# First batch scored in two halves, an expert order by landing, and a last part stored in four pieces

## The chip, the cores and the metric

The kernel runs on one core of a Trainium2 chip. The core has TensorE (matmuls; its weight loads are listed apart as PEld), VectorE (DVE), ScalarE (ACT), GpSimd (POOL) and SyncE (SP, which here only issues transfers), and sixteen DMA engines that carry every transfer. The metric is the device time in microseconds, the median over runs.

## The reference

Two stages, all in float32. The first is an attention between 512 tokens and 32 states for 8 batches of 8 heads (head size 64), in both directions: `softmax(x state^T / 8) state` gives the tokens' read, `softmax(state x^T / 8) x` the states' read. The two are joined to 544 rows a batch, 4352 rows of 512 in all. The second stage is a soft mixture of 8 experts with 4 slots each: `logits = rows @ phi` (512 x 32); a softmax down the rows gives the slots' inputs; each expert does `max(slot @ w1, 0) @ w2` (512 to 1024 to 512) on its 4 slots; a softmax along the 32 logits mixes the slots' outputs back to every row. The weights are 33.6 MB of the input, x is 8.4 MB, and 8.9 MB are written.

## The kernel before

The program is one list of steps, `ORDER`, that is walked once; each word is a function and its arguments (`X.2.1` is `X(2, 1)`), and a `!` has its copy done by VectorE, not ScalarE. The engines' instruction queues follow this list, so it alone sets what stands ahead of what. `HOMES` names the buffer that each tile takes in turn, and with it which older reader a transfer must wait for.

Attention, for batch b. `X` (L317) turns the x of two heads on TensorE, four blocks of 128 x 128, `xe` copies them out scaled, `S` (L330) scores all heads against the states into two banks, `sp0` and `sp1`. From there two ways run side by side. `q`, `m1`, `sub`, `x1`, `l1`, `rr`, `mul`, `aT` turn the scores (VectorE), take maxima (VectorE), subtract (GpSimd), exponentiate (ScalarE), sum (VectorE), divide (GpSimd) and turn back (VectorE): the tokens' softmax. `m2`, `e2`, `E`, `ee`, `R` do the states' softmax and its product with x. `A`/`ae` turn the tokens' softmax for later, `Lx` makes its logits `lt`.

Slots' inputs, for a pair of batches k: `mx`, `mk`, `bm`, `nme` find the running maximum, `dx` exponentiates, `dT`/`dTe` turn the result, `T`, `tt`, `Px`, `Y` add the pair's share to `y`. For the states' rows `Ls`, `Lr`, `msx`, `dsx`, `Ps`, `Ys` do the same, with `V`/`Ve` and `U`/`Ue` turning what they need; `keep` and `lkp` copy logits aside. At the end `SI` turns `y` and `SIe` writes the slots' inputs to `si_m` (L723).

Experts. `W.hf.e` (L744) is expert e's first layer for one half of the 1024 columns, four matmuls, each of which stands twice in the trace; eight of them add up in one bank. `hc`, `ht`, `hr` copy, turn and sum it. `u.k.hf.e` (L804) is the second layer for output part k of 128 columns; parts 0, 1 use the first column half of w2 and parts 2, 3 the second. `c`, `s` sum a part, `o` (L836) mixes it back to rows, `oc` (L851) copies the eight banks of a part out, four by each engine, and stores each four banks as 1 MB:

```python
n = 2 if (k, q) in HALVED else 4
if j % n == n - 1:
```

Transfers. ScalarE issues one of the first three; SP issues all others in the order of the list, into one queue. Weights land in the order of `LOADS`: most of the first layer's tiles early, with those of experts 3 and 4 of the first half taken late because their buffers still hold attention data (steps `ld`), then the second layer's. The stores follow in the same queue.

Of the kernel before, what the change touches and what calls it, by code (L numbers as in the profile page):

```python
# [52 lines left out]
srTe.6 A.5.1 windows aT.6.0 mk.2 l1.7.1 A.5.0 bm.2 nme.2 ae.5.0 R.7.0 ae.5.1 Lx.6.0 rr.7 mul.7.0 aT.6.1 R.7.1 sr.7
dx.2 A.6.0 dT.2 dTe.2! srT.7 aT.7.0 A.6.1 keep.2 mul.7.1 aT.7.1 pv.3! srTe.7 Ls.1 tt.1 D.0 T.2 Lx.6.1 Lx.7.0 Lx.7.1
mx.3 mk.3! ld.4 als.0 ld.5 ae.6.0 al.2 ae.6.1 V.1 A.7.0 bm.3 nme.3 ae.7.0! A.7.1 al.1 Lse.1 Lr.1 msx.1 dx.3 dT.3
dTe.3! al.3 ae.7.1 Px.1 Lu.1 Lus.0 Lu.2 als.1 tt.2 Ps.0 Ue.1 dsx.1 T.3 Px.2 Lu.3 Lus.1 Y.1 Ys.0 ld.6 D.1 ld.7 ld.8
# [868 lines left out]
```

## Time and profile before

| | us |
|---|---|
| median of 3 runs (lowest to highest) | 131.38 (131.15 to 132.03) |
| profiled execution | 131.39 |
| its span, first to last instruction | 129.6 |
| TensorE busy | 116.3 (90%) |
| VectorE, ScalarE, GpSimd busy | 87.4, 74.2, 44.3 |
| moved by the DMA engines | 51.76 MB, mean 399 GB/s |

The span is what the profiler saw of the program, and 1.8 us of the time lie around it. A busy share is a mean over stages that have different limits, so the tables by stretch say more than this one. For a transfer two times matter: when it is issued, and when it has landed, which is what a waiting instruction sees.

### The profile page before, as it was taken

To read this page: it belongs to the slowest core of one execution; us is meant where nothing else is said; L and a number is where in the kernel's file an instruction comes from. 1 tells how busy PE (TensorE), PEld (TensorE's weight loads), DVE (VectorE), ACT (ScalarE), POOL (GpSimd) and SP (SyncE) were. 2 spreads that over 40 slices of the span, in tenths; PEclk is the share of its full clock that TensorE was granted. 3 is DMA by queue.
4 is the path that set the end of the run, shared out by engine and by line. 5 is a ranking of instruction groups with operands and counts; after the bars stand their busy time and mean duration, and the time that the engine had idled before them with its cause. 6 is when DMAs were issued, how large, how long until landed. Compare 5 with 4: busy or idle time off the path is not lost.

```text
span 129.6 us, 4822 instructions
## 1 busy us (share of the span) xinstructions
PE 116.3 (90%) x2064; PEld 81.4 (63%) x2064; DVE 87.4 (67%) x200; ACT 74.2 (57%) x180; POOL 44.3 (34%) x60
## 2 busy tenths in 40 slices
PE   6999999999996999999999987999999999998300
PEld 3655969688665869677888672334694659476000
DVE  3049999999999999999986746049083653352700
ACT  3039999999996999999938410121203571342500
POOL 2103348563669083596664115503330000000000
PEclk9999999999999999999999999999999999999985
DMA  4999999999999999999999999999999999989593
GB/s 103 365 382 465 425 405 435 440 415 448 417 410 455 420 410 445 397 425 427 450 422 420 410 410 411 425 430 430 427 430 445 382 408 412 426 362 397 217 410 164
DMA packets 7078, 51.76 MB, mean 399 GB/s; under 512 B 784, under 2 KB 912, under 8 KB 3216
## 3 DMA queue, kind: packets, MB, share of 16 engines
q1 hardware_dynamic: 6912, 50.92, 94.4%
q10 hardware_dynamic: 144, 0.52, 1.1%
q8 instruction: 16, 0.26, 0.7%
q14 instruction: 6, 0.05, 0.1%
HBM read 42.53 MB, written 8.91 MB: 397 GB/s over the span
## 4 chain that ended last, share of the span: by engine, by line
PE 77%; DMA 12%; DVE 2%; issue 2%; ACT 1%; DVEq 0%
PE xt_ps L320 12%; DMA w<-w_in 12%; PE so_ps L813 11%; PE h_ps L750 8%; PE o L842 7%; PE sr_ps L422 7%; PE eT_ps L397 7%; PE sc L334 6%; PE an_ps L397 4%; PE spin L286 3%; PE lt L452 3%; DVE out L262 1%; PE sum_ps L832 1%; PE os L864 1%; PE hT_ps L766 1%
## 5 line engine op out<-in xcount | busy, mean ns | idle before, releaser
L356 POOL TENSOR_TENSOR q<-q,m 128x512 f32<-128x512 f32 x16 | 16.7, 1049 | 23.2 <-DVE m L352 12.4
L265 ACT ACTIVATE xt<-xt_ps 128x512 f32<-128x512 f32 x30 | 17.0, 616 | 6.3 <-PE xt_ps L320 6.3
L373 POOL TENSOR_TENSOR q<-q,rr 128x512 f32<-128x512 f32 x16 | 16.6, 1049 | 4.2 <-ACT e L389 1.9
L750 PE MATMUL h_ps<-w,si_m 128*32 128x512 f32 x128 | 14.8, 594 | 1.0 <-DMA w<-w_in 0.7
L320 PE MATMUL xt_ps<-ident,x 128*128 128x128 f32 x112 | 15.6, 276 | 0.0
L813 PE MATMUL so_ps<-w,h_m 128*32 128x128 f32 x432 | 14.3, 274 | 0.0
L813 PEld LDWEIGHTS so_ps<-w,h_m 128*32 128x32 f32 x432 | 11.7, 110 | 3.7 <-issue 3.1
L320 PEld LDWEIGHTS xt_ps<-ident,x 128*128 128x128 f32 x112 | 12.5, 141 | 1.6 <-DMA x<-x_in 0.8
L262 DVE COPY out<-o 128x512 f32<-128x512 f32 x15 | 9.4, 685 | 5.4 <-PE o L842 5.4
L384 DVE TENSOR_REDUCE nm<-sc 128x1 f32<-128x512 f32 x16 | 10.6, 663 | 1.5 <-PE sc L334 1.5
L389 ACT ACTIVATE e<-sc,nm 128x512 f32<-128x512 f32 x16 | 11.4, 723 | 0.1
L842 PE MATMUL o<-lt_all,so_r 32*128 32x512 f32 x64 | 11.2, 615 | 0.0
L262 ACT COPY out<-o 128x512 f32<-128x512 f32 x17 | 8.9, 597 | 4.0 <-PE o L842 4.0
L347 DVE STREAM_TRANSPOSE q<-sc 128x512 f32<-128x512 f32 x16 | 11.0, 692 | 0.2 <-PE sc L334 0.2
L397 PE MATMUL eT_ps<-ident,e 128*128 128x128 f32 x64 | 10.2, 281 | 1.0 <-issue 0.9
L397 PEld LDWEIGHTS eT_ps<-ident,e 128*128 128x128 f32 x64 | 7.0, 140 | 6.2 <-ACT e L389 4.2
L378 DVE STREAM_TRANSPOSE aT<-q 128x512 f32<-128x512 f32 x16 | 10.7, 687 | 0.3
L750 PEld LDWEIGHTS h_ps<-w,si_m 128*32 128x32 f32 x128 | 5.7, 110 | 7.9 <-issue 5.3
L359 ACT ACTIVATE q<-q 128x512 f32<-128x512 f32 x16 | 10.6, 660 | 0.0
L352 DVE TENSOR_REDUCE m<-q 128x16 f32<-128x512 f32 x16 | 10.5, 663 | 0.0
L362 DVE TENSOR_REDUCE ls<-q 128x16 f32<-128x512 f32 x16 | 10.4, 653 | 0.0
L262 ACT COPY eT<-eT_ps 128x512 f32<-128x512 f32 x16 | 9.6, 606 | 1.3 <-PE eT_ps L397 1.2
(138 smaller groups left out, 198.0 us busy)
## 6 DMA issues: line engine op xcount, KB each, us to landing
...
w<-w_in SPq DMA_DIRECT2D x9, 1024.0 KB, 15.1
out_x<-out SPq DMA_DIRECT2D x7, 1024.0 KB, 7.0
...
x<-x_in SPq DMA_DIRECT2D x2, 1024.0 KB, 14.6
x<-x_in SPq DMA_DIRECT2D x2, 512.0 KB, 7.1
w_half<-w_in SPq DMA_DIRECT2D x4, 256.0 KB, 15.5
w_an<-w_in SPq DMA_DIRECT2D x2, 512.0 KB, 10.6
```

The lines of the kernel that those rows point to most:

```text
L262: (dve.tensor_copy if Z["dve"] else act.copy)(out, in_)
L265: (dve.tensor_scalar_mul if Z["dve"] else act.mul)(out, in_, by)
L320: pe.transpose(p[:, P * j : P * j + P], xg[b, g][:, j, :], ident)
L347: dve.transpose(r[f"q{h}"], r[f"sp{h}"])
L356: pool.tensor_tensor(v, v, R[b][f"m1{h}"].broadcast_to([P, 16, NS]), op=ALU.subtract)
L373: pool.tensor_tensor(v, v, R[b]["rr"][:, 16 * h : 16 * h + 16].broadcast_to([P, 16, NS]), op=ALU.mult)
L378: dve.transpose(r[f"aT{h}"], r[f"q{h}"])
L389: act.activation(r[f"e2{h}"], r[f"sp{h}"], AF.Exp, bias=r[f"nm2{h}"], accum_out=ls[:, b % 2, 32 + h, 0:1])
L397: pe.transpose(p[:, j, :], r[f"{src}{h}"][:, P * j : P * j + P], ident)
L750: pe.matmul(h_ps[hf][32 * kt : 32 * kt + 32, :], si_m[kt // 2][:, 256 * (kt % 2) + 32 * e : 256 * (kt % 2) + 32 * e + 32], wt[1, hf, e, kt ...
L813: pe.matmul(so[k][32 * i : 32 * i + 32, :], h_m[hf][:, 256 * i + 32 * e : 256 * i + 32 * e + 32], wt[2, c, e, 4 * hf + i][:, col : col + n ...
L842: pe.matmul(o[j], so_r[hf][rows, col : col + 128], lt_all[rows, 4 * q : 4 * q + 4, :].rearrange("p b s -> p (b s)"), start=True, stop=True,)
```

## The change

The first batch's input is laid out by halves of 256 tokens: SP loads the states' head and groups 0 and 1 of the first half, ScalarE groups 2 and 3 of it, SP the second half. New steps `Xa`, `xa`, `Sa`, `qa`, `ma`, `sa` turn, scale, score, turn, reduce and subtract a half t at a time. `w1_part` counts the experts that are left, so that they may come in any order, and experts 3 and 4 of the first half come last. The last output part is stored in four pieces of 512 KB. The three turns that kept TensorE busy ahead of `SI` (`spin.3`) stand at the end. The list of steps and the buffers' turns are new throughout.

```diff
@@ ORDER, the list of steps: its start, the first expert layer, its end
-X.0.0 xe.0.0! X.0.2 X.0.1 X.0.3 xe.0.2 xe.0.3 xe.0.1! S.0 X.1.0 xe.1.0 m2.0.0 q.0.1 q.0.0 X.1.1 xe.1.1 X.1.2 m1.0.1
+Xa.0.1 xa.0.1! Xa.0.0 xa.0.0 Xa.1.1 xa.1.1! Xa.1.0 xa.1.0 Sa.0 qa.0.0 ma.0.0 Sa.1 qa.1.0 X.1.1 xe.1.1 X.1.0 xe.1.0
...
-tt.3 Y.2 Wd We Ve.1 Ps.1 Px.3 Y.3 Ys.1 spin.3 SI SIe W.0.0 W.0.1 lkp.1 W.0.2 W.0.3 W.0.4 W.0.5 cm.2 W.0.6 W.0.7
+Ys.1 SI We SIe W.0.0 cm.0 W.0.1 W.0.2 W.0.5 ld.8 ld.9 ld.10 W.0.6 W.0.7 W.0.3 ld.11 cx.0 W.0.4 hc.0 W.1.0 lkp.1!
...
+oc.3.1.0 oc.3.1.1! oc.3.1.2 oc.3.1.3! spin.3
...
-HALVED = ((0, 0),)
+HALVED = ((0, 0), (3, 0), (3, 1))
...
-    first = 2 * NJ * D
     xs_a = big_tile("x0_a")
     xs_b = big_tile("x0_b")
-    stT_sb = xs_b[:, first : first + 8 * P].rearrange("p (q g a b n) -> p q g a b n", q=4, g=2, a=2, b=2)
+    stT_sb = xs_b[:, F:].rearrange("p (q g a b n) -> p q g a b n", q=4, g=2, a=2, b=2)
     phi_sb = cp.tile([P, 4, NS], F32, name="phi_sb")
-    head = first + 2 * P
+    quarter, head = 4 * P, 6 * P
     nc.sync.dma_start(xs_a[:, 0:head], x0[:, 0:head])
-    act.dma_start(xs_a[:, head : head + 2 * first], x0[:, head : head + 2 * first])
-    nc.sync.dma_start(xs_b[:, 0:first], x0[:, head + 2 * first :])
-    st_head = xs_a[:, first : first + 2 * P].rearrange("p (g a b n) -> p g a b n", g=2, a=2, b=2)
+    act.dma_start(xs_a[:, head : head + quarter], x0[:, head : head + quarter])
+    nc.sync.dma_start(xs_b[:, 0:F], x0[:, head + quarter :])
+    st_head = xs_a[:, quarter:head].rearrange("p (g a b n) -> p g a b n", g=2, a=2, b=2)
+    x0_half = [
+        [t.rearrange("p (g j c) -> p g j c", g=2, j=2) for t in (xs_a[:, 0:quarter], xs_a[:, head : head + quarter])],
+        [t.rearrange("p (g j c) -> p g j c", g=2, j=2) for t in (xs_b[:, 0:quarter], xs_b[:, quarter:F])],
+    ]
     xg = {}
-    for g, t in enumerate((xs_a, xs_a[:, head:], xs_a[:, head + first :], xs_b)):
-        xg[0, g] = t[:, 0:first].rearrange("p (j c) -> p j c", j=NJ)
+
+    def x_at(b, g, j):
+        return xg[b, g][:, j] if b else x0_half[j // 2][g // 2][:, g % 2, j % 2]
+
...
+        def Xa(t, p):
+            r = R[0]
+            r[f"xp{t}{p}"] = x = bank([P, S], f"xt_ps0_{t}{p}")
+            for i in range(4):
+                pe.transpose(x[:, P * i : P * i + P], x_at(0, 2 * p + i // 2, 2 * t + i % 2), ident)
+
+        def xa(t, p):
+            r = R[0]
+            r[f"xt{t}{p}"] = half(f"xt0_{t}{p}")
+            scale(r[f"xt{t}{p}"], r[f"xp{t}{p}"], 0.125)
+
+        def Sa(t):
+            r = R[0]
+            n = S // 2
+            for h in range(2):
+                if t == 0:
+                    r[f"sp{h}"] = bank([P, S], f"sc0_{h}")
+            for g in range(4):
+                for h in range(2):
+                    pe.matmul(
+                        r[f"sp{h}"][32 * g : 32 * g + 32, n * t : n * t + n],
+                        st_t(0, g)[64 * h : 64 * h + 64, :],
+                        r[f"xt{t}{g // 2}"][64 * h : 64 * h + 64, n * (g % 2) : n * (g % 2) + n],
+                        start=True,
+                        stop=True,
+                    )
+
+        def qa(t, h):
+            r = R[0]
+            if t == 0:
+                r[f"q{h}"] = half(f"q0_{h}")
+                r[f"qv{h}"] = r[f"q{h}"].rearrange("p (k n) -> p k n", n=NS)
+                r[f"m1{h}"] = sm.tile([P, 16, 1], F32, tag=f"m1{h}", name=f"m1_0_{h}")
+            c = slice(S // 2 * t, S // 2 * (t + 1))
+            dve.transpose(r[f"q{h}"][:, c], r[f"sp{h}"][:, c])
+
+        def ma(t, h):
+            r = R[0]
+            k = slice(8 * t, 8 * t + 8)
+            dve.tensor_reduce(out=r[f"m1{h}"][:, k], in_=r[f"qv{h}"][:, k], axis=AX.X, op=ALU.max)
+
+        def sa(t, h):
+            r = R[0]
+            k = slice(8 * t, 8 * t + 8)
+            v = r[f"qv{h}"][:, k]
+            pool.tensor_tensor(v, v, r[f"m1{h}"][:, k].broadcast_to([P, 8, NS]), op=ALU.subtract)
...
-            if e == 0:
+            i0 = h_ps[hf] is None
+            if i0:
                 h_ps[hf] = bank([P, 512], f"h_ps{hf}")
+            w1_left[hf] -= 1
             for kt in range(4):
                 pe.matmul(
                     h_ps[hf][32 * kt : 32 * kt + 32, :],
                     si_m[kt // 2][:, 256 * (kt % 2) + 32 * e : 256 * (kt % 2) + 32 * e + 32],
                     wt[1, hf, e, kt],
-                    start=(e == 0),
-                    stop=(e == E - 1),
+                    start=i0,
+                    stop=(w1_left[hf] == 0),
                 )
...
+    x0 = xs[0].reshape(P, 4, 2, 2 * P).transpose(0, 2, 1, 3).reshape(P, 2, F)
-        "x0_in": con(_np.concatenate([xs[0, :, 0:512], sts[:, 0:256], xs[0, :, 512:]], axis=1)),
+        "x0_in": con(_np.concatenate([x0[:, 0, 0:512], sts[:, 0:256], x0[:, 0, 512:], x0[:, 1]], axis=1)),
```

Nearly all rows of the list differ; three places are shown as they were built. On TensorE the program starts with the first batch (`xt_ps` are turns, `sc` scores; x0_a and x0_b hold its input). Before:

```order
L320 MATMUL xt_ps0_0_138<-ident_87,x0_a_66 128x128 x4
L320 MATMUL xt_ps0_2_145<-ident_87,x0_a_66 128x128 x4
L320 MATMUL xt_ps0_1_150<-ident_87,x0_a_66 128x128 x4
L320 MATMUL xt_ps0_3_155<-ident_87,x0_b_67 128x128 x4
L334 MATMUL sc0_0_166<-xt0_0_143,x0_a_66 32x512
L334 MATMUL sc0_1_167<-xt0_0_143,x0_a_66 32x512
L334 MATMUL sc0_0_166<-xt0_1_164,x0_a_66 32x512
L334 MATMUL sc0_1_167<-xt0_1_164,x0_a_66 32x512
```

Now:

```order
L391 MATMUL xt_ps0_01_138<-ident_87,x0_a_66 128x128 x4
L391 MATMUL xt_ps0_00_145<-ident_87,x0_a_66 128x128 x4
L391 MATMUL xt_ps0_11_152<-ident_87,x0_b_67 128x128 x4
L391 MATMUL xt_ps0_10_159<-ident_87,x0_b_67 128x128 x4
L406 MATMUL sc0_0_166<-xt0_00_150,x0_a_66 32x256
L406 MATMUL sc0_1_167<-xt0_00_150,x0_a_66 32x256
L406 MATMUL sc0_0_166<-xt0_00_150,x0_a_66 32x256
L406 MATMUL sc0_1_167<-xt0_00_150,x0_a_66 32x256
```

The four turns still stand ahead of the scores, and the scores now go by 256 tokens, the first half for all groups before the second.

On TensorE at the first expert layer (`w_3276800`, `w_3538944`, `w_3801088` are experts 0 to 2, `w_5111808` and `w_5373952` experts 3 and 4, `w_0` and `w_524288` experts 5 to 7), before, from expert 2 on:

```order
L750 MATMUL h_ps0_1616<-w_3801088_756,si_m0_1319 32x512 x2
L750 MATMUL h_ps0_1616<-w_3801088_756,si_m1_1321 32x512 x2
L750 MATMUL h_ps0_1616<-w_5111808_1457,si_m0_1319 32x512 x2
L750 MATMUL h_ps0_1616<-w_5111808_1457,si_m1_1321 32x512 x2
L750 MATMUL h_ps0_1616<-w_5373952_1564,si_m0_1319 32x512 x2
L750 MATMUL h_ps0_1616<-w_5373952_1564,si_m1_1321 32x512 x2
L750 MATMUL h_ps0_1616<-w_0_124,si_m0_1319 32x512 x2
L750 MATMUL h_ps0_1616<-w_0_124,si_m1_1321 32x512 x2
L750 MATMUL h_ps0_1616<-w_0_124,si_m0_1319 32x512 x2
L750 MATMUL h_ps0_1616<-w_0_124,si_m1_1321 32x512 x2
L750 MATMUL h_ps0_1616<-w_524288_126,si_m0_1319 32x512 x2
L750 MATMUL h_ps0_1616<-w_524288_126,si_m1_1321 32x512 x2
```

Now:

```order
L805 MATMUL h_ps0_1623<-w_3801088_1227,si_m0_1458 32x512 x2
L805 MATMUL h_ps0_1623<-w_3801088_1227,si_m1_1460 32x512 x2
L805 MATMUL h_ps0_1623<-w_0_124,si_m0_1458 32x512 x2
L805 MATMUL h_ps0_1623<-w_0_124,si_m1_1460 32x512 x2
L805 MATMUL h_ps0_1623<-w_0_124,si_m0_1458 32x512 x2
L805 MATMUL h_ps0_1623<-w_0_124,si_m1_1460 32x512 x2
L805 MATMUL h_ps0_1623<-w_524288_126,si_m0_1458 32x512 x2
L805 MATMUL h_ps0_1623<-w_524288_126,si_m1_1460 32x512 x2
L805 MATMUL h_ps0_1623<-w_5111808_1539,si_m0_1458 32x512 x2
L805 MATMUL h_ps0_1623<-w_5111808_1539,si_m1_1460 32x512 x2
L805 MATMUL h_ps0_1623<-w_5373952_1589,si_m0_1458 32x512 x2
L805 MATMUL h_ps0_1623<-w_5373952_1589,si_m1_1460 32x512 x2
```

Experts 3 and 4 have moved behind 5, 6 and 7.

On VectorE at the end of the attention, from the last transpose of the tokens' softmax on (`an` and `lt` are copies out of banks, `mx` the last pair's maximum), before:

```order
L378 STREAM_TRANSPOSE aT7_1_1408<-q7_1_1123 128x512
L265 TENSOR_SCALAR mk_3_1410<-nm_all_105 128x1
L580 STREAM_TRANSPOSE tt_1_1418<-t_ps1_1181 128x128
L665 STREAM_TRANSPOSE D0_1420<-ds0_1304 128x32
L468 TENSOR_REDUCE mx_3_1451<-lt_6_1355 128x1
L265 TENSOR_SCALAR mk_3_1410<-mask_97,mx_3_1451 128x4
L532 TENSOR_REDUCE nm_all_105<-bm_ps3_1473 128x1
L262 COPY an7_1476<-an_ps7_0_1468 128x16x32
L644 TENSOR_REDUCE lr1_1486<-lr1_1486 128x1
L500 TENSOR_TENSOR nm_all_105<-lr1_1486,nm_all_105 128x1
L262 COPY dT_3_1500<-dT_ps3_1497 128x256
```

Now:

```order
L384 STREAM_TRANSPOSE aT7_1_1414<-q7_1_1166 128x512
L268 COPY an6_1436<-an_ps6_0_1400 128x16x32
L268 COPY lt_all_103<-lt_6_1438 128x256
L521 TENSOR_REDUCE mx_3_1475<-lt_6_1438 128x1
L268 COPY an7_1483<-an_ps7_0_1470 128x16x32
L585 TENSOR_REDUCE nm_all_105<-bm_ps3_1485 128x1
L268 COPY an7_1483<-an_ps7_1_1478 128x16x32
L633 STREAM_TRANSPOSE tt_2_1503<-t_ps2_1417 128x128
L577 SCALAR_TENSOR_TENSOR y_85<-y_85,al_all_106,px_ps1_1494 128x128
L268 COPY srN1_1531<-v_ps1_1465 128x512
L697 TENSOR_REDUCE lr1_1533<-lr1_1533 128x1
L553 TENSOR_TENSOR nm_all_105<-lr1_1533,nm_all_105 128x1
```

Copies of an6 and lt stand between that transpose and the maximum now, two of an7 around the running maximum, and one of srN after it; two of dT are gone from this engine.

## Rows read from the trace of the kernel before

**Rows 1.** the page, part 2: DMA share in 40 slices, in tenths.

```profile
DMA  4999999999999999999999999999999999989593
```

**Rows 2.** windows: us, busy time of each engine, PEclk, DMA share, GB/s.

```profile
10.00:15.00 5.00, 5.00 (x62) 3.56 (x61) 5.00 (x11) 5.00 (x12) 2.10 (x2) 1.00 1.05 447
...
75.00:80.00 5.00, 4.07 (x33) 2.82 (x32) 3.31 (x11) 0.42 (x1) 1.26 (x3) 1.00 1.01 408
```

**Rows 3.** timeline of PE at the first expert layer: start, us, what.

```profile
75.44 3.91 PE L750 MATMUL h_ps<-w,si_m 128*32 128x512 f32 x32 [0.28 <-DVE si_m L723]
...
80.10 5.36 PE L750 MATMUL h_ps<-w,si_m 128*32 128x512 f32 x48 [0.74 <-DMA w<-w_in]
```

**Rows 4.** chain of waits, whole span: start, us, what.

```profile
64.99 15.07 DMA w<-w_in
```

**Rows 5.** timeline of the first batch's scores and their first reader.

```profile
7.52 1.81 PE L334 MATMUL sc<-xt,x_a 64*32 64x512 f32 x16
...
9.36 0.69 DVE L384 TENSOR_REDUCE nm<-sc 128x1 f32<-128x512 f32 x1 [1.47 <-PE sc L334]
```

**Rows 6.** groups by line and form: busy, mean ns, idle before.

```profile
L347 DVE STREAM_TRANSPOSE q<-sc 128x512 f32<-128x512 f32 x16 | 11.0, 692 | 0.2 <-PE sc L334 0.2
...
L304 DVE STREAM_TRANSPOSE G_sb<-g_ps 128x256 f32<-128x256 f32 x2 | 0.8, 423 | 0.0
...
L262 DVE COPY an<-an_ps 128x512 f32<-128x512 f32 x2 | 1.4, 680 | 0.0
...
L262 DVE COPY dT<-dT_ps 128x256 f32<-128x256 f32 x2 | 0.8, 419 | 0.3 <-PE dT_ps L555 0.3
```

**Rows 7.** timeline of DVE at the end of the attention.

```profile
68.25 0.42 DVE L468 TENSOR_REDUCE mx<-lt 128x1 f32<-128x256 f32 x1 [0.25 <-PE lt L452]
...
75.20 0.48 DVE L723 TENSOR_TENSOR si_m<-si_ps,rl 128x32 f32<-128x32 f32 x4 [0.48 <-PE si_ps L705]
```

**Rows 8.** the last load: issue, us to landing; then PE's column-1 run.

```profile
87.10 0.33 SPq L201 DMA_DIRECT2D w<-w_in  x1
...
w<-w_in SPq DMA_DIRECT2D x1, 512.0 KB, 18.7
...
106.94 2.83 PE L813 MATMUL so_ps<-w,h_m 128*32 128x128 f32 x96
```

**Rows 9.** chain of waits, from 117 us to the end.

```profile
117.26 0.30 DVE so_sb L262
...
118.99 1.13 PE o L842 x6
...
120.12 1.27 DVE out L262 x2
```

**Rows 10.** timeline of SP, the last stores' issues.

```profile
119.75 0.33 SPq L873 DMA_DIRECT2D out_s<-out_s  x1
...
121.84 1.15 SPq L857 DMA_DIRECT2D out_x<-out  x2
```

**Rows 11.** DMA issues from 119.75, 121.84 and 122.66: size, us to landing.

```profile
out_s<-out_s SPq DMA_DIRECT2D x1, 256.0 KB, 3.0
...
out_x<-out SPq DMA_DIRECT2D x1, 1024.0 KB, 4.4
...
out_x<-out SPq DMA_DIRECT2D x1, 1024.0 KB, 6.0
```

**Rows 12.** windows around the last stores' start, columns as before.

```profile
121.50:122.00 0.50, 0.00 (x0) 0.00 (x0) 0.50 (x2) 0.23 (x1) 0.00 (x0) 1.00 0.14 53
...
122.40:122.60 0.20, 0.00 (x0) 0.00 (x0) 0.19 (x1) 0.00 (x0) 0.00 (x0) 1.00 0.00 0
...
122.60:122.80 0.20, 0.00 (x0) 0.00 (x0) 0.00 (x0) 0.00 (x0) 0.00 (x0) 1.00 1.25 532
```

**Rows 13.** windows while 512 KB and while 1 MB stores move.

```profile
109.00:110.00 1.00, 1.00 (x44) 1.00 (x40) 0.00 (x0) 0.00 (x0) 0.00 (x0) 1.00 1.07 434
...
115.00:116.00 1.00, 1.00 (x46) 1.00 (x40) 0.05 (x1) 0.06 (x1) 0.00 (x0) 1.00 1.03 434
```

More of the change, by code (lines that the diff above doesn't have):

```diff
@@ L53 @@
[L53 to L56, printed above, removed]
-tt.3 Y.2 Wd We Ve.1 Ps.1 Px.3 Y.3 Ys.1 spin.3 SI SIe W.0.0 W.0.1 lkp.1 W.0.2 W.0.3 W.0.4 W.0.5 cm.2 W.0.6 W.0.7
@@ new lines @@
+qa.0.1 ma.1.0 sa.0.0 sa.1.0 X.1.3 xe.1.3 m2.0.1 X.1.2 qa.1.1 ma.0.1 xe.1.2 ma.1.1 m2.0.0 U.0 sa.0.1 S.1 sa.1.1
+x1.0.0 l1.0.0 m2.1.1 q.1.0 G.0 e2.0.1 E.0.1 e2.0.0 x1.0.1 m2.1.0 m1.1.0 sub.1.0 ee.0.1 X.2.0 xe.2.0 X.2.3 xe.2.3
+E.0.0 ee.0.0 l1.0.1 q.1.1 rr.0 X.2.1 mul.0.1 xe.2.1 m1.1.1 X.2.2 xe.2.2 R.0.0 e2.1.0 Ge.0 e2.1.1 Ue.0 R.0.1 sr.0 S.2
+m2.2.1 x1.1.0 aT.0.1 E.1.0 ee.1.0 e2.2.1 m2.2.0 E.1.1 X.3.1 X.3.2 xe.3.1 xe.3.2 q.2.0 X.3.3 xe.3.3 m1.2.0 sub.1.1
+E.2.1 X.3.0 mul.0.0 aT.0.0 xe.3.0 q.2.1 srT.0 l1.1.0 x1.1.1 ld.0 l1.1.1 R.1.0 m1.2.1 sub.2.0 S.3 m2.3.0 sub.2.1
@@ new lines @@
+X.4.1 rr.1 e2.2.0 E.2.0 ee.2.1 ee.1.1 ee.2.0 xe.4.1 q.3.0 m2.3.1 Lx.0.0 srTe.0 x1.2.1 R.1.1 sr.1 mul.1.0 aT.1.0
+m1.3.0 mul.1.1 aT.1.1 sub.3.0 Lx.0.1 R.2.0 x1.2.0 A.0.1 X.4.0 A.0.0 e2.3.0 e2.3.1 ae.0.0 X.4.3 xe.4.3 srT.1 srTe.1!
+q.3.1 R.2.1 Lx.1.0 Lx.1.1 ae.0.1 xe.4.0 E.3.1 mx.0 m1.3.1 l1.2.0 mk.0 X.4.2 xe.4.2 A.1.0 X.5.0 keep.0 sub.3.1 l1.2.1
+rr.2 ld.1 sr.2 bm.0 nme.0 x1.3.0 S.4 ae.1.0 x1.3.1 l1.3.0 dx.0 l1.3.1 E.3.0 mul.2.0 aT.2.0 ee.3.0 X.5.1 xe.5.1
+ee.3.1 X.5.2 xe.5.2 A.1.1 dT.0 m2.4.1 X.5.3 rr.3 srT.2 m2.4.0 q.4.1 mul.3.0 m1.4.1 R.3.0 mul.3.1 R.3.1 sub.4.1
@@ new lines @@
+xe.5.0 xe.5.3 S.5 ae.1.1 dTe.0 e2.4.0 T.0 srTe.2 A.2.0 aT.3.0 q.4.0 e2.4.1 E.4.1 x1.4.1 sr.3 srT.3 mul.2.1 srTe.3
+X.6.3 ee.4.1 X.6.1 A.3.0 ae.2.0 al.0 m1.4.0 X.6.2 E.4.0 q.5.0 xe.6.1 aT.3.1 m2.5.1 tt.0 sub.4.0 x1.4.0 A.3.1 Lx.2.0
+aT.2.1 ae.3.0 ee.4.0 Lx.2.1 R.4.0 R.4.1 m1.5.0 sub.5.0 l1.4.0 q.5.1 xe.6.3 l1.4.1 rr.4 pv.1! x1.5.0 X.6.0 m1.5.1
+Lx.3.0 xe.6.2 xe.6.0 ae.3.1 sr.4 Lx.3.1 e2.5.1 Ls.0 Lse.0 S.6 mul.4.1 Px.0 E.5.1 m2.5.0 aT.4.1 e2.5.0 mx.1 ee.5.1
+mk.1 X.7.3 Y.0 E.5.0 A.2.1 ee.5.0 q.6.0 sub.5.1 x1.5.1 m2.6.0 q.6.1 l1.5.0 xe.7.3 ae.2.1 X.7.2 l1.5.1 R.5.0 R.5.1
@@ new lines @@
+mul.4.0 aT.4.0 keep.1 xe.7.2 m2.6.1 X.7.1 xe.7.1 m1.6.1 sub.6.1 X.7.0 xe.7.0 bm.1 nme.1 dx.1 Lr.0 rr.5 msx.0 m1.6.0
+e2.6.0 mul.5.0 S.7 q.7.0 srT.4 e2.6.1 dT.1 m2.7.0 m2.7.1 E.6.0 dTe.1 E.6.1 dsx.0 q.7.1 ee.6.0 mul.5.1 aT.5.0 m1.7.1
+sr.5 V.0 ee.6.1 Ve.0 R.6.0 aT.5.1 Lx.4.0 R.6.1 x1.6.1 ld.2 sub.6.0 x1.6.0 e2.7.1 srTe.4 sub.7.1 e2.7.0 x1.7.1 T.1
+m1.7.0 ld.3 als.0 Lx.4.1 Lx.5.0 Lx.5.1 srT.5 srTe.5 E.7.0 pv.2! tt.1 E.7.1 l1.6.0 A.5.0 ee.7.0 sub.7.0 A.4.0 mx.2
+mk.2 bm.2 l1.6.1 rr.6 A.5.1 D.0 mul.6.0 Lu.0 x1.7.0 lkp.0 ae.4.0 ee.7.1 nme.2 ae.5.0 sr.6 l1.7.0 l1.7.1 rr.7 srT.6
@@ new lines @@
+aT.6.0 R.7.0 R.7.1 sr.7 keep.2 dx.2 srTe.6! mul.6.1 A.4.1 dT.2 aT.6.1 pv.3 U.1 A.6.0 srT.7 mul.7.0 ae.5.1 dTe.2
+aT.7.0 mul.7.1 aT.7.1 ae.4.1 T.2 ld.4 ae.6.0! Lx.6.0 Lx.6.1 Lx.7.0 Lx.7.1 keep.3! al.1 al.2 windows Lu.1 srTe.7 V.1
+A.7.0 mx.3 mk.3 A.7.1 ae.7.0! bm.3 nme.3 Lus.0 dx.3 ae.7.1! Px.1 tt.2 Ue.1 Ps.0 Ls.1 Lse.1 A.6.1 ae.6.1 dT.3 dTe.3
+Y.1 Ve.1! Lr.1 ld.5 Lu.2 al.3 msx.1 als.1 Px.2 Ys.0 dsx.1 D.1 T.3 Ps.1 tt.3 Lu.3 Y.2 ld.6 ld.7 Px.3 Lus.1 Wd Y.3
+Ys.1 SI We SIe W.0.0 cm.0 W.0.1 W.0.2 W.0.5 ld.8 ld.9 ld.10 W.0.6 W.0.7 W.0.3 ld.11 cx.0 W.0.4 hc.0 W.1.0 lkp.1!
@@ new lines @@
+cm.2 cd.0 ht.0 cm.1 ld.12 cx.1 cb.0 hz W.1.1 W.1.2 hr.0 u.1.0.0 u.1.0.1 u.1.0.2 W.1.3 W.1.4 W.1.5 W.1.6 W.1.7 hc.1
+u.0.0.0 u.0.0.1 u.0.0.2 cd.1 u.1.0.3 ht.1 u.1.0.4 cx.2 hr.1 u.0.0.3 u.0.0.4 u.0.0.5 ld.13 u.0.0.6 u.0.0.7 u.0.1.0
+u.0.1.1 cb.1 u.0.1.2 u.0.1.3 u.1.0.5 ld.14 u.0.1.4 u.0.1.5 u.0.1.6 u.0.1.7 u.1.0.6 u.1.0.7 c.0 s.0 u.1.1.0 o.0.0!
+u.1.1.1 ld.15 oc.0.0.0 o.0.1 cd.2 cb.2 u.1.1.2 u.1.1.3 u.1.1.4 u.1.1.5 u.1.1.6 u.1.1.7 oc.0.1.0 oc.0.1.1 oc.0.1.2
+oc.0.1.3 oc.0.0.1! c.1! u.2.0.0 u.2.0.1 oc.0.0.2 oc.0.0.3! s.1 os.0 o.1.0! u.3.0.0 oc.1.0.0 oc.1.0.1! u.2.0.2
@@ new lines @@
+u.3.0.1 u.2.0.3 oc.1.0.2 oc.1.0.3! o.1.1 oc.1.1.0! oc.1.1.1 oc.1.1.2! u.2.0.4 u.2.0.5 u.2.0.6 u.2.0.7 u.2.1.0
+oc.1.1.3 u.2.1.1 u.2.1.2 u.2.1.3 u.2.1.4 u.2.1.5 u.2.1.6 u.2.1.7 c.2 u.3.0.2 u.3.0.3 s.2! u.3.0.4 o.2.0 oc.2.0.0
+oc.2.0.1! oc.2.0.2 oc.2.0.3! u.3.0.5 o.2.1 oc.2.1.0 oc.2.1.1! u.3.0.6 u.3.0.7 u.3.1.0 oc.2.1.2! u.3.1.1 u.3.1.2
+u.3.1.3 u.3.1.4 u.3.1.5 u.3.1.6 u.3.1.7 c.3! oc.2.1.3 s.3! os.1 o.3.0! o.3.1! oc.3.0.0! oc.3.0.1 oc.3.0.2 oc.3.0.3!
+oc.3.1.0 oc.3.1.1! oc.3.1.2 oc.3.1.3! spin.3
@@ L70 @@
     big="""
-0 1 2 3 4 0 2 3 1 4 0 2 3 1 4
+0 1 2 3 4 0 2 3 4 1 0 2 3 4 1
 """,
@@ L319, in X @@
             for j in range(NJ):
-                pe.transpose(p[:, P * j : P * j + P], xg[b, g][:, j, :], ident)
+                pe.transpose(p[:, P * j : P * j + P], x_at(b, g, j), ident)
         def xe(b, g):
@@ L736, in attention_soft_moe @@
         )
-        h_ps = [None, None]
+        h_ps, w1_left = [None, None], [E, E]
         h_m, h_sb, hT = [None, None], [None, None], [None, None]
```

39 lines of the change are left out of this document (5 added, 34 removed), and 8 rows, old and new, of the table b.

## The prediction

> **What bounds the kernel now.** I read the page's DMA line first [rows 1]: from the second slice of 3.2 us on, the sixteen DMA engines are busy 9 tenths or more, and they fall off only in the last five slices. The windows say what stands beside that. In 10 to 15 us VectorE and ScalarE are full (5.00 of 5.00 us) and TensorE's clock is granted in full, 1.00, which is the level of 2.4 GHz; in 75 to 80 us VectorE, ScalarE and GpSimd are half idle and TensorE works 4.07 of 5 us, while the DMA share is still 1.01 [rows 2]. So there are two clocks in this kernel. One is the compute: attention until 75, then experts. The other is one stream of bytes, loads first and stores behind them, on engines that hardly rest between 3 and 113 us. The reader should ask of each part of the change which of the two it moves.
>
> The chain of waits at the seam is a load: issued at 64.99, landed at 80.06 [rows 4]. TensorE's timeline shows what hung on it: 32 matmuls of the first expert layer from 75.44 on, then 0.74 us of idle until that load, then 48 more without a stop [rows 3]. The last load is issued at 87.10 and lands 18.7 us later, at 105.8; TensorE reads its column half of the second layer from 106.94 on [rows 8], a slack of 1.1 us. From there the chain goes over TensorE to the last expert at 117.26, the last products from 118.99 and VectorE's last copies from 120.12 [rows 9], and to the two stores of 1 MB issued from 121.84 on [rows 10]. The second is issued 0.33 us before that row's end, at 122.66, and lands 6.0 us later, at 128.7 [rows 10, 11]. The span ends 0.9 us behind it.
>
> **The change part by part.** The sum is made against the profiled execution: span 129.6 us, 131.39 us in all, 0.01 over the median of 131.38.
>
> *First batch in halves.* The bytes are the same. TensorE must now turn both halves before it scores the first (Sa.0 stands behind Xa.1.0), so the score starts about when it did, at 7.3 to 7.5, but its first half is half of the old 1.81 us [rows 5]: VectorE can start near 8.3 instead of 9.36, by this estimate 1.1 us earlier. It then pays for four more instructions (the four that become eight): a transpose of 256 columns takes 423 ns against 692 for 512 [rows 6], so two transposes that become four cost 4 x 0.423 - 2 x 0.692 = 0.31 us, and the two maxima, taken alike, another 0.31. That leaves 0.5 us of lead on an engine that is full from there to the end of the attention. On GpSimd two subtractions become four, at an engine that is busy 2.10 of 5 us [rows 2].
>
> *New order of the attention.* Nearly every step stands elsewhere; the total per engine hardly changes. One place can be priced. Between the last attention transpose and the maximum of the last group, VectorE now has two copies that were on ScalarE or later: one of an_ps (0.68 [rows 6]) and the 256-column copy of lt (0.42). In the old order that maximum, at 68.25, followed 0.25 us of idle [rows 7], so the cover is thin and at least 0.42 lies on the path that ends with si_m at 75.20 [rows 7]. I set lead and toll against each other: between +0.5 and -1.5, taken as zero, since the start's gain is nearly the toll's size.
>
> *Late experts last.* The tiles of experts 3 and 4 land last. Before, expert 4 stood fifth and TensorE waited 0.74 us for it; now three experts that landed long ago stand between, at 5.36/6 = 0.89 us each [rows 3]. From 75.44 on, seven experts take to 81.7, and expert 4 has landed at 80.06. The stall goes: 0.74 by the row of idle, 80.10 - 75.44 - 4 x 0.89 = 1.1 by the pace of the later run. I take 0.9. What is late next is the last load: with 0.9 less, TensorE would come to the second column half at 106.0, still behind 105.8, and the tile of that last load is for expert 7, which stands after parts for seven others. So it does not wait there.
>
> *Four stores instead of two.* The first 512 KB need two copies, one on each engine, instead of four: VectorE's first ends near 120.75 [rows 9], so its store can go near 120.9 instead of 121.84, 1.0 us earlier. Each store adds an issue of 0.33 us on SP [rows 10], which has nothing else to do. Whether smaller stores move slower: while halves of 512 KB moved the DMA took 434 GB/s, and while full ones moved 434 [rows 13]. I take zero; the bounds are zero and one more issue each, 0.7. The Trainium skill (DMA: Bandwidth & Descriptors, Rules for kernel authors) asks for at least 1 MiB per DMA for full bandwidth, which speaks against this split; the equal rates here do not bear it out for 512 KB, and by it the gain below would only shrink.
>
> *The three warm-up turns* go from before the experts to the very end of PE's queue. There si_m waited for VectorE, not for them; at the end nobody waits for them.
>
> *The sum.* On the compute's clock: 0.9 + 1.0 = 1.9 us earlier first store of the last part. But the DMA engines must be free for it. The out_s store issued at 119.75, a quarter of a megabyte, needed 3.0 us and landed at 122.75; the next megabyte, issued at 121.84, landed at 126.2, 3.5 us later [rows 11], where 1 MB takes 2.4 us at 434 GB/s. So at most 1.0 to 1.1 us of the slowest engine's time can be won. The windows bound it from below: the share is 0.14 from 121.5 on, zero only in 122.4 to 122.6, and full again behind 122.6 [rows 12]. A few engines were still working off old stores until about 122.3, and for these the pause was 0.4 us. The gain is between 0.4 and 1.1; I take 0.8, nearer the landings, because a landing is what ends the run. 131.39 - 0.8 = **130.6 us**, against the median the same.
>
> The Trainium skill (Perfetto Trace Analysis, DMA Optimizations) says that splitting transfers lets the task end sooner if DMA engines are generally idle. The share near 1.0 up to 113 us and the pause of 0.4 us agree with reading it as a limit here.
>
> **The rivals.** *The compute's clock is the only one.* If the laggard engines are less behind in the new run, because stores two and three come earlier too and nothing is refilled late, all 1.9 us pass: 129.5, and 129.2 with a part of the lead. For it: in 121.5 to 122 most engines were idle (0.14). Against it: the few that were not decide a landing. It decides if out_s lands before about 121.7 instead of 122.75. Chance 0.20.
>
> *The new order makes the expert layer late.* In the last 8 us of attention VectorE now has copies of an three times (0.68 each), of lt (0.42) and of v's result (0.68), 3.1 us, where it had one of an and two of dT, 1.5 us [rows 6]. ScalarE has three copies ahead of the last dT, estimated at 0.5 each from the same rows. If all of this lies on the chain to si_m, that is 1.6 + 1.5 = 3.1 us, the first store goes at 121.84 - 1.9 + 3.1 = 123.0, and with 6.85 us from issue to the last landing, as before, the end is 1.2 later: 132.6. It costs from the point at which si_m is later than 75.2 by more than 1.9 us. For it: the old chain there had half a microsecond of idle at each link and no more. Against it: work before that point got lighter by the same copies. Chance 0.13.
>
> *Nothing is won.* The stall goes but SP's issues, smaller rows and an engine that lags as before eat it: 131.2 to 131.5. Chance 0.14. The forecast has the rest, 0.53, with its own range of 130.2 to 131.0.
>
> **How the numbers follow.** A time within 1% of 131.38 (130.07 to 132.69) can't be told from no change by these measurements. Faster by over 1%: nearly all of the first rival and a tail of the forecast, 0.18 + 0.08 = 0.26. Slower by over 1%: the larger part of the second, 0.10. The rest, 0.64, is the same. The range is 129.4 to 132.2: it leaves out the lower edge of the first rival and the upper part of the second.
>
> **What would show it.** Right: no idle of TensorE ahead of a matmul of h_ps; VectorE's first score transpose near 8; si_m within 1 us of 75.2; last loads landing at 105 to 106 as before; four stores from about 120 on, and between the landing of out_s and the last landing no pause, so that the end is 4.9 us behind out_s. The DMA share has no window at zero before the last store. Wrong: si_m later than 77; a new wait for a load in the second layer; or an out_s that lands below 122, which means that the engines' lag was not fixed and the first rival holds.

## The result and the profile after

The changed kernel took 130.12 us (median of 10 runs, 129.82 to 130.58) against 131.19 us of the kernel before, measured again beside it: a ratio of 0.9918 (95% interval 0.9895 to 0.9941), 1.07 us less. A second measurement, beside three of the kernels below, gave 0.9896 (0.9867 to 0.9926). The profiled execution that is read here is the longest of the ten: it took 130.58 us, with a span of 128.8.

The page's DMA line after, in 40 slices of 3.2 us; it answers to [rows 1]:

```profile
DMA  4999999999999999999999999999999999999991
```

The fall in the last five slices is gone: the sixteen DMA engines are busy up to the last slice. Two windows around the last stores say the same (columns as in [rows 12]):

```profile
121.50:122.00 0.50, 0.00 (x0) 0.00 (x0) 0.07 (x1) 0.00 (x0) 0.00 (x0) 1.00 1.05 426
...
122.40:122.60 0.20, 0.00 (x0) 0.00 (x0) 0.00 (x0) 0.00 (x0) 0.00 (x0) 0.50 1.20 492
```

Where the share was 0.14 and then zero, it is 1.05 and 1.20; the lowest half microsecond between 119 and 124 us has 0.61. The stores of the last part are now issued by SP (start, us, count) at

```profile
119.08 0.34 SPq L928 DMA_DIRECT2D out_s<-out_s  x1
120.04 2.77 SPq L912 DMA_DIRECT2D out_x<-out  x4
```

and the transfers issued at 119.08 and, as the last of the four, at 121.82 land after (size, us from issue to landing)

```profile
out_s<-out_s SPq DMA_DIRECT2D x1, 256.0 KB, 3.8
...
out_x<-out SPq DMA_DIRECT2D x1, 512.0 KB, 5.8
```

So the first store of the last part goes 1.8 us earlier than in [rows 10] (120.04 for 121.84), but out_s lands at 122.88, where it landed before (122.79), and the last landing is at 127.66 instead of 128.67: 1.0 us. TensorE and VectorE at the two places that the prediction named, start and length first:

```profile
8.98 0.67 PE L406 MATMUL sc<-xt,x_a 64*32 64x256 f32 x16 [0.69 <-DVE q L421]
...
76.29 8.21 PE L805 MATMUL h_ps<-w,si_m 128*32 128x512 f32 x72 [0.42 <-DVE si_m L776]
```

```profile
8.38 0.45 DVE L421 STREAM_TRANSPOSE q<-sc 128x256 f32<-128x256 f32 x1 [0.39 <-PE sc L406]
...
76.04 0.49 DVE L776 TENSOR_TENSOR si_m<-si_ps,rl 128x32 f32<-128x32 f32 x4
```

The idle for a load in the expert layer [rows 3] is gone: 72 matmul records in one piece (each product stands twice in the trace). VectorE turns the first scores at 8.38 (its first reading of them was at 9.36, [rows 5]). And `si_m` is 0.84 us later than in [rows 7].

### The profile page after: what moved, and what is told of

Same layout as the page of the kernel before. It is cut to its first block, busy times and chain, and to the rows that moved or that the text cites. A ratio compares the mean times of both kernels' runs of the same rounds, so it can differ in the third digit from the quotient of the medians.

```text
span 128.8 us, 4863 instructions
## 1 busy us (share of the span) xinstructions
PE 115.7 (90%) x2080; PEld 83.6 (65%) x2080; DVE 88.6 (69%) x206; ACT 74.1 (58%) x178; POOL 44.7 (35%) x62
## 4 chain that ended last, share of the span: by engine, by line
PE 54%; DVE 17%; ACT 16%; issue 5%; POOL 2%; DVEq 1%; POOLq 0%
PE so_ps L868 12%; PE h_ps L805 11%; PE o L897 7%; ACT xt L271 4%; PE spin L292 3%; ACT q L365 3%; DVE nm L437 3%; PE sc L340 3%; DVE q L353 3%; ACT e L442 2%; DVE m L358 2%; ACT eT L268 2%; DVE aT L384 2%; PE an_ps L450 2%; ACT an L268 2%
## 5 line engine op out<-in xcount | busy, mean ns | idle before, releaser
L362 POOL TENSOR_TENSOR q<-q,m 128x512 f32<-128x512 f32 x14 | 14.7, 1049 | 15.7 <-DVE m L358 9.2
L868 PE MATMUL so_ps<-w,h_m 128*32 128x128 f32 x432 | 15.1, 275 | 0.0
L268 ACT COPY out<-o 128x512 f32<-128x512 f32 x18 | 9.5, 596 | 7.4 <-PE o L897 7.4
L805 PEld LDWEIGHTS h_ps<-w,si_m 128*32 128x32 f32 x128 | 8.6, 110 | 4.1 <-issue 3.2
L897 PE MATMUL o<-lt_all,so_r 32*128 32x512 f32 x64 | 10.3, 629 | 0.0
L353 DVE STREAM_TRANSPOSE q<-sc 128x512 f32<-128x512 f32 x14 | 9.8, 697 | 0.1
L450 PE MATMUL eT_ps<-ident,e 128*128 128x128 f32 x64 | 9.7, 280 | 0.0
L450 PE MATMUL an_ps<-ident,aT 128*128 128x128 f32 x64 | 9.5, 277 | 0.0
L358 DVE TENSOR_REDUCE m<-q 128x16 f32<-128x512 f32 x14 | 9.2, 661 | 0.1
```

The costliest lines, as they stand in the source:

```text
L268: (dve.tensor_copy if Z["dve"] else act.copy)(out, in_)
L362: pool.tensor_tensor(v, v, R[b][f"m1{h}"].broadcast_to([P, 16, NS]), op=ALU.subtract)
L450: pe.transpose(p[:, j, :], r[f"{src}{h}"][:, P * j : P * j + P], ident)
L805: pe.matmul(h_ps[hf][32 * kt : 32 * kt + 32, :], si_m[kt // 2][:, 256 * (kt % 2) + 32 * e : 256 * (kt % 2) + 32 * e + 32], wt[1, hf, e, kt ...
L868: pe.matmul(so[k][32 * i : 32 * i + 32, :], h_m[hf][:, 256 * i + 32 * e : 256 * i + 32 * e + 32], wt[2, c, e, 4 * hf + i][:, col : col + n ...
L897: pe.matmul(o[j], so_r[hf][rows, col : col + 128], lt_all[rows, 4 * q : 4 * q + 4, :].rearrange("p b s -> p (b s)"), start=True, stop=True,)
```

## Experiments

Two theories stood against each other. In the forecast, called the stream theory below, the DMA engines' stream sets the end (by the slowest of the sixteen engines), and time won by the products counts only while that stream has a pause. In its rival, the compute theory, every part's gain reaches the end and the parts add.

**The parts, one by one.** Four kernels took the change apart.

```diff
# a1: before
-HALVED = ((0, 0),)
+HALVED = ((0, 0), (3, 0), (3, 1))
# a2: before, with w1_part as in the change
-W.0.0 W.0.1 lkp.1 W.0.2 W.0.3 W.0.4 W.0.5 cm.2 W.0.6 W.0.7
+W.0.0 W.0.1 lkp.1 W.0.2 W.0.5 W.0.6 W.0.7 cm.2 W.0.3 W.0.4
# a3: before, with both
# a4: the change, without both
-HALVED = ((0, 0), (3, 0), (3, 1))
+HALVED = ((0, 0),)
-W.0.2 W.0.5 ld.8 ld.9 ld.10 W.0.6 W.0.7 W.0.3 ld.11 cx.0 W.0.4
+W.0.2 W.0.3 ld.8 ld.9 ld.10 W.0.4 W.0.5 W.0.6 ld.11 cx.0 W.0.7
```

a1, stores alone. 

> The kernel before with the last part in four stores of 512 KB and nothing else. Stream theory (the forecast: the slowest DMA engine sets the end, and what a part wins counts only until that engine has no pause left): the first store of the last part goes near 120.9 instead of 121.84, the pause behind out_s (1.0 us on the slowest engine) closes, and the end is 0.8 to 1.0 us earlier: nearly the whole gain of the change by itself, ratio 0.992 to 0.994. Compute theory (the parts add, each by the time it takes from the products' clock): half of the measured 1.1, ratio 0.995 to 0.997. Small rows are slow: no gain, 0.999 to 1.003.

a2, late experts alone. 

> The kernel before with experts 3 and 4 taken last in the first half of the first layer and nothing else. The wait of 0.74 us for expert 4 goes, all later products come 0.7 to 0.9 earlier. Stream theory: the stores of 1 MB go at 121.0 and 121.8 instead of 121.84 and 122.66, out_s lands near 122.7 as before, and the end is 0.7 to 0.9 earlier, ratio 0.993 to 0.995. Compute theory: 0.4 to 0.5 of the measured 1.1, ratio 0.996 to 0.997. A third: the wait only moves to another load, ratio 0.999 to 1.001, and the trace shows an idle of TensorE ahead of a later product.

a3, both. 

> The kernel before with both the four stores and experts 3 and 4 last, in the old order of the attention and the old loads at the start. Stream theory: no more than either alone, since the slowest engine's pause is only 1.0 us: ratio 0.991 to 0.993, the time of the change itself, although the first store goes near 120.0. Compute theory: 1.7 us earlier, ratio 0.986 to 0.988. If the new attention order costs something in the change, this kernel is faster than the change by that.

a4, neither. 

> The changed kernel with both undone: stores of 1 MB and experts in order; what is left is the first batch in halves and the new order of attention and products. In the change the first products of the expert layer came 0.85 us later than before (76.29 for 75.44), but the products of the output came apart in pairs and made that good (last products at 118.31 for 118.99 with the stall gone). Stream theory: TensorE waits 0.3 us for expert 4, last products near 118.6, first store near 121.5: some 0.3 to 0.8 earlier, ratio 0.994 to 0.998. The attention order as a loss: 0.85 later, ratio 1.003 to 1.007. Compute theory: 0.3 to 0.4, ratio 0.997.

Measured, as ratios to before: a1 0.9967 (0.9951 to 0.9982), a2 0.9938 (0.9908 to 0.9969), a3 0.9945 (0.9919 to 0.9971), a4 0.9938 (0.9918 to 0.9959). The stores alone won less than the stream theory gave them and fell where the compute theory had them. a2's ratio is one that the stream theory gave, but its interval reaches both. a3 and a4 speak against the compute theory, whose ratios lie outside their intervals, though a3 won a little less than the stream theory had and a4 a little more: both edits together won no more than the late experts alone, and the new order without either won as much. The three single gains sum to 1.6% (0.33, 0.62, 0.62), and the whole change won 0.8 to 1.0%. The intervals are 0.3 to 0.6% wide, so the sum speaks for parts that don't add, without proving it; the runs below are sharper.

TensorE's timeline at the expert layer shows the late-expert edit apart from the rest. First a2, then a4:

```profile
75.65 7.91 PE L752 MATMUL h_ps<-w,si_m 128*32 128x512 f32 x69 [0.28 <-DVE si_m L723]
```

```profile
75.36 3.91 PE L805 MATMUL h_ps<-w,si_m 128*32 128x512 f32 x32 [0.42 <-DVE si_m L776]
80.29 3.21 PE L805 MATMUL h_ps<-w,si_m 128*32 128x512 f32 x28 [1.01 <-DMA w<-w_in]
```

In a2 no idle is left; in a4 the wait for expert 4 is back, with 1.01 us. It is the longer the earlier `si_m` is, because the load lands when it lands: 0.74 us in before, 0.97 in b4 and 1.25 in a1, where the first product goes at 75.44, 75.38 and 74.82 and the load has landed near 80 in all of them.

**Fewer bytes.**

```diff
# b1 in the change, b4 in before
+if (k, q) != (1, 1):
     nc.sync.dma_start(out_x[k, q][:, part], ...)
```

b1, the change. 

> The changed kernel without the store of 1 MB of part (1, 1), which is never written; nothing else differs, and no engine waits for that store. Stream theory: the slowest engine reaches out_s 2.4 us earlier, so the last four stores move as soon as they are issued: from 120.04 with 1.2 us until the first byte and 4 x 1.24 us, an end near 126.3 instead of 127.7, 1.3 us below the change, ratio to before 0.981 to 0.984. Compute theory: the end hangs on the last copies, which do not move: ratio 0.990 to 0.993, as the change.

b4, before. 

> The kernel before without the store of 1 MB of part (1, 1). Stream theory: in before the slowest engine already paused ahead of the last two stores, so 2.4 us less of stream bring only what lag that engine still had at the end: 0.72 us between the first and the last of its sixteen landings, ratio 0.994 to 0.997. If the bytes alone set the time: 2.4 us, ratio 0.982. If the products alone: 1.000.

b1: 0.990 (0.988 to 0.9919). b4: 0.9997 (0.9982 to 1.0012). Both went against the stream theory as I had put it, and both fell where the compute theory had them (0.990 to 0.993 and 1.000): a megabyte less, 2.4 us of stream, bought the change some 0.2 us and before nothing. For b4 that means that before did not end by its stream at all. b1 has out_s issued at 118.46, and it landed after

```profile
out_s<-out_s SPq DMA_DIRECT2D x1, 256.0 KB, 3.6
```

that is at 122.09, only 0.8 us before the change's. A transfer's landing stands in the trace as sixteen shares, which I take to be one of each engine. Fifteen of them were there at 120.51 (in the change at 122.03); the last one came 1.58 us later. So the missing megabyte freed fifteen engines and not the slowest. The end, 126.99, is 4.90 us behind that landing, as the forecast had it. What else stood at nearly the same place, the next runs say.

**A later last part.** These kernels make products of the last part more than once, between out_s and the first store.

```diff
# b2 (DELAY 4) and b3 (DELAY 12), in the change
-for j in range(NJ):
+for j in [0] * (DELAY if (k, q) == (3, 0) else 0) + list(range(NJ)):
# c2, in the change
-for j in range(NJ):
+for j in list(range(NJ)) * (2 if (k, q) == (3, 0) else 1):
```

b2. 

> The changed kernel with the first product of the last part (3, 0) made five times instead of once, ahead of that part's other products and behind those of out_s: four repeats, about 1.1 us on TensorE by 1.14 us for a group of four. Stream theory: the last part's first store goes at 121.1 instead of 120.0, its first byte could move at 122.3, and the slowest engine is busy until 122.9: no loss or nearly none, ratio to before 0.991 to 0.995. Compute theory: 1.1 us later than the change, ratio 0.999 to 1.002.

b3. 

> As the run with four repeats, but twelve of them: about 3.4 us. Stream theory: the first store goes at 123.4, its first byte at 124.6, 1.8 us behind the point at which the slowest engine is free; the end is 1.5 to 1.9 later than the change, ratio to before 1.003 to 1.007. Compute theory: 3.4 later, ratio 1.016 to 1.019.

b2 took 1.0117 (1.0092 to 1.0142) and b3 1.1176 (1.1141 to 1.1210). The delays were mis-sized, so these two decide nothing between the theories: b2's first store went at 124.17, about 3.2 us late by its out_s (issued at 120.04, where the change has 0.96 us between the two), and b3's at 137.50. (b2's profiled execution took 134.18 us where four others took 132.35 to 132.81; its expert layer began late, at 77.25.) Repeats of one product are dear, which the last section tells. They gave a number all the same. With the DMA engines idle by then, the last landing came 7.02 us behind the first store in both (131.19 - 124.17, 144.52 - 137.50). That is what four stores of 512 KB need when nothing is ahead of them; I call it the drain. (The expectations of b1 to b3 count 1.2 us from an issue to its first byte, which no run shows: in b3, with the engines idle, the DMA share is zero up to 138.3 and 1.03 in the next 0.2 us, 0.8 us behind the issue.)

From this, after those runs, came the drain theory: **the end is the later of two times**, the first store plus the drain, and the stream's own end. c2 repeats the delay with four products on four different groups of rows. It was run with c1 (the change, with `HALVED` back to `((0, 0),)`), c3 (all halves in stores of 512 KB, `HALVED = tuple((k, q) for k in range(4) for q in range(2))`) and c4, the change as it is.

c1. 

> The changed kernel with the last part in two stores of 1 MB again; start, attention and experts stay as changed. Drain theory (formed after the last runs: the end is the later of two times, the first store of the last part plus 6.8 to 7.0 us, and the slowest DMA engine, which in the change is 0.6 us behind that): the first store goes at 120.9 instead of 120.04, which with 6.85 gives 127.75 for 127.66, 0.1 later; ratio to before 0.991 to 0.994. Compute theory: 0.85 later, ratio 0.998. Stream theory: as the change, 0.992.

c2. 

> The changed kernel with the four products of the last part's first half made twice in their own order, so that they overlap as they do once: 1.14 us on TensorE ahead of the last part, out_s untouched. Drain theory: 0.6 of it is slack, so 0.5 later than the change, ratio to before 0.994 to 0.998. Compute theory: 1.1 later, ratio 1.000. Stream theory: not later, 0.992. If the repeats cost more than 1.14 (as the repeats of one product did), the issue of the first store says how much.

c3. 

> The changed kernel with every half of every part in stores of 512 KB: five stores of 1 MB become ten. By 1.22 to 1.24 us for 512 KB and 2.44 for 1 MB in the change's landings the rows cost nothing or 0.04 per MB, 0.2 us in all, on an engine with 0.6 us over the drain: ratio 0.991 to 0.995. Should halves be clearly slower than 1 MB (a tenth less, as a rule of at least 1 MB per transfer would suggest), 5 MB lose 1.2 us: ratio 1.001.

c4. 

> The changed kernel as it is, for a time on the same chip as the three beside it and a second profile. Ratio 0.989 to 0.995. If the 0.85 us by which its expert layer began later than before was a loss of the new attention order, the first product of the expert layer stands near 76.3 again; if it was chance of one execution, it stands between 74.8 and 76.3 as in the others.

c1 0.9934 (0.9897 to 0.9971), c2 0.9916 (0.9885 to 0.9947), c3 0.9889 (0.9858 to 0.9920), c4 0.9896 (0.9867 to 0.9926), all on one chip. c1 and c4 are where the drain theory had them, and c3 is just below its range. c2 missed its range (0.994 to 0.998) and came out as the stream theory had it; but that range was made for a delay of 1.14 us with 0.6 of it free, and the delay was smaller. The compute theory's ratios for c1 and c2 lie outside the intervals, c1's narrowly. c2 beside c4 is the sharpest pair. SP's rows of c4, and the transfer of its last store, issued at 120.81:

```profile
118.08 0.34 SPq L928 DMA_DIRECT2D out_s<-out_s  x1
119.03 2.77 SPq L912 DMA_DIRECT2D out_x<-out  x4
```

```profile
out_x<-out SPq DMA_DIRECT2D x1, 512.0 KB, 6.5
```

The same of c2, whose last store is issued at 122.49:

```profile
118.89 0.34 SPq L928 DMA_DIRECT2D out_s<-out_s  x1
120.70 2.77 SPq L912 DMA_DIRECT2D out_x<-out  x4
```

```profile
out_x<-out SPq DMA_DIRECT2D x1, 512.0 KB, 5.2
```

c2 issues 1.81 us behind its out_s instead of 0.95, so the delay is 0.86 us. By the compute theory that is 0.66%, a ratio of 0.996, outside c2's interval, or 130.89 us, above all six of c2's times (129.93 to 130.86); it cost 0.15 us in the medians (130.18 for 130.03), which can't be told from nothing, nor from the 0.26 that the drain theory leaves of 0.86. Between these two executions the first store moved by 1.67 us and the last landing by 0.43 (127.29 to 127.72): the transfer waits out the difference in the queue, 6.5 us instead of 5.2. In c4 the stream runs on while nothing is left to compute:

```profile
121.00:122.00 1.00, 0.00 (x0) 0.00 (x0) 0.00 (x0) 0.00 (x0) 0.00 (x0) 1.00 1.03 416
```

All kernels against the rule. F is the issue of the last part's first store, L the landing of the last load, both from the trace. Behind L come 8.5 MB of stores, seventeen times 512 KB at 1.24 us (c4's last three landings are 124.80, 126.05 and 127.29), or 21.1 us. I take 21.0, which is c4's own time from L to its last landing, so c4's row doesn't test it. In b1 and b4 it is 7.5 MB, 18.6 us. For the drain I take 6.9, between before's 6.83 and the 7.02.

| kernel | F | L | F + 6.9 | L + 21.0 | last landing |
|---|---|---|---|---|---|
| before | 121.84 | 105.84 | 128.7 | 126.8 | 128.67 |
| a1 stores alone | 121.14 | 105.85 | 128.0 | 126.9 | 127.68 |
| a2 late experts alone | 120.72 | 106.61 | 127.6 | 127.6 | 127.70 |
| a3 both | 119.56 | 106.29 | 126.5 | 127.3 | 127.24 |
| a4 neither | 121.04 | 106.60 | 127.9 | 127.6 | 127.91 |
| the change | 120.04 | 105.94 | 126.9 | 126.9 | 127.66 |
| c4 the change again | 119.03 | 106.27 | 125.9 | 127.3 | 127.29 |
| c1 two stores | 119.99 | 106.14 | 126.9 | 127.1 | 127.06 |
| c2 delay | 120.70 | 105.93 | 127.6 | 126.9 | 127.72 |
| c3 all halves | 120.06 | 105.54 | 127.0 | 126.5 | 126.84 |
| b1 change, 1 MB less | 119.44 | 105.88 | 126.3 | 124.5 | 126.99 |
| b4 before, 1 MB less | 121.62 | 106.33 | 128.5 | 124.9 | 128.54 |

The later of the two is within 0.4 us of the last landing in ten of twelve. Before ended by its drain, 1.9 us behind its stream; the change has the two within a microsecond of each other, and in c4 the stream is the later one. That is why a part alone may win much and the next part little, and why neither a megabyte less (b1) nor 0.86 us more of products (c2) moves the change by more than 0.2 us. The change's own profile and b1 lie 0.7 us above the rule: there one of the sixteen engines ended behind the others (in b1 its share of the last store landed 1.4 us behind the first, in b3, with nothing ahead, 0.87).

For these two the forecast's own sign does better. It had the end 4.9 us behind the landing of out_s, which is the landing of its slowest share. Measured it is 4.8 to 5.2 in the ten kernels other than before and b4, where it is 5.88 and 5.69 and the drain sets the end. With that time in place of L + 21.0 the later of the two is within 0.12 us of the last landing in eleven of twelve kernels, the change and b1 among them (a1 is 0.36 off). So the slowest engine, and not the bytes alone, is the second clock. What puts it behind was not tried. In b1 its lag grows from 0.55 us at the store that lands at 117.78 to 1.65 at the one that lands at 121.47, and a 16 KB read of instructions, which the trace has among the engines' packets, starts at 117.24 and takes 0.96; that the one makes the other is not shown.

## Why the prediction was right

The time forecast was 130.6 from 131.38, a ratio of 0.994, and 130.12 came, 0.992: in the range of 129.4 to 132.2, just under the likeliest case's own (130.2 to 131.0), and within 1% of before, as given most of the chance. Of the 0.5 us between, 0.2 is the kernel before, which took 131.19 this time, and 0.3 the gain, 1.07 for 0.8. By its steps:

*What bounds the kernel.* Right: two clocks. The trace of the change has the signs that were listed: no window at zero, four stores from 120.04, the last landing 4.8 us behind out_s (4.9 forecast), out_s not below 122, `si_m` within 1 us of 75.2. c2 shows that the products' clock no longer sets the end alone.

*Late experts last, 0.9.* Right. From the first product of the expert layer to the sums of the last part TensorE needed 42.26 us in before (75.44 to 117.70) and 41.30 in a2 and in a3, which differ from it there by that edit alone: 0.96. Of this 0.74 is the wait itself and 0.22 stands beside it. In a1 and b4, which have the old expert order, it was 42.77 and 42.48 with their longer waits, so what the edit is worth depends on when `si_m` comes.

*Four stores, 1.0.* Too much. From those sums to the first store it was 4.14 us before (121.84 - 117.70) and 3.07 in the change (120.04 - 116.97), 1.07 less; the sums of before and of the change:

```profile
117.70 0.46 PE L832 MATMUL sum_ps<-so_sb,rep 128*128 128x128 f32 x2 [0.51 <-DVE so_sb L262]
```

```profile
116.97 0.49 PE L887 MATMUL sum_ps<-so_sb,rep 128*128 128x128 f32 x2 [0.41 <-DVE so_sb L268]
```

But the pairs that differ by the stores alone show half of it: 0.59 in a1 against before (3.55 for 4.14), 0.60 in a3 against a2 (3.17 for 3.77), 0.49 in c4 against c1 (3.07 for 3.56). Another 0.37 is the new order, which the sum did not have: VectorE's first copy of the last part starts 2.40 us behind the sums in before, a1 and a2 (120.10 in before) and 2.03 in the change and c1.

*Smaller rows cost nothing.* Right for 512 KB: c3, with ten more of them in place of five of 1 MB, took 129.89 us beside c4's 130.03. c3's last four stores landed 1.21 to 1.27 us apart. The Trainium skill (DMA: Bandwidth & Descriptors, Rules for kernel authors) asks for 1 MiB and more per DMA for the highest bandwidth; no run here shows a loss at 512 KB.

*First batch and new order of the attention, taken as zero.* Mis-sized, within its bounds. VectorE started at 8.38, as forecast (8.3), but its lead did not last (its transposes and maxima of these scores are done at 12.98 instead of 13.03): the second half's scores waited 0.69 us for VectorE's reading of the first half, in the row from 8.98 above. Both halves of a score lie in one bank. The Trainium skill (PSUM — Partial Sum Buffer, PSUM bank collisions raise a hardware error) says that two engines must not be in one bank and partition at once, so that software orders them; the trace agrees with such an order. The first product of the expert layer stands at 74.8 to 75.7 in the five profiles with the old attention (mean 75.28), at 75.3 to 77.3 in nine with the new (75.94): 0.66 us later, or 0.50 without b2, the latest. c4, the change again, has 75.28, as the old ones. One profile each and a spread wider than the difference, so the size is rough; its sign is that of the second rival, at a fifth of the 3.1 us which that had as its bound.

*What the sum did not have.* The order of the second layer. With the wait gone, the way to the last sums is 41.30 us in a2 and 40.68 in the change and in c4: 0.62 less. (a1 and a4, less their waits of 1.25 and 1.01, differ by 0.63.) In the new list products of other parts stand between the two halves of an output. Before (one row of its timeline), then the change:

```profile
98.29 2.92 PE L842 MATMUL o<-lt_all,so_r 32*128 32x512 f32 x16
```

```profile
97.98 1.14 PE L897 MATMUL o<-lt_all,so_r 32*128 32x512 f32 x8
...
99.41 1.49 PE L897 MATMUL o<-lt_all,so_r 32*128 32x512 f32 x8
```

Sixteen records at a stretch take 2.92 us, two eights 2.63, and something like it stands at three parts. By their rows the three make 0.9, more than the 0.62, so the order costs something elsewhere; no run of its own tried it. The misses cancel: 0.96 + 1.07 + 0.62 - 0.66 = 1.99 us on the products' clock, where 1.9 were forecast and 1.80 stand in the profiled execution. That the forecast's 1.9 came out is luck: the stores gave 0.5 to 0.6 of their 1.0, and the new order, taken as nothing, won 0.37 and 0.62 and lost some 0.5 to 0.7.

*The DMA limit, 0.8 of that.* Right in kind, and in size at the upper of its bounds (0.4 to 1.1): 1.07 measured (0.8 to 1.4 by the interval). Its picture was too simple. I took engines that still work off old stores as the only limit. b1 shows that a megabyte less of old stores hardly helps: the slowest engine stays late without it, and the drain (126.3) is not far behind.

*The rivals.* The compute's clock alone (129.5) fell with c2 and with out_s, which landed at 122.88. The late expert layer came at a fifth of its price. That nothing is won lies outside the interval.
